# Attention values as paired 64-row matmuls in four accumulator banks, score and value units one by one, projection as one unit a block

## The chip, the cores and the metric

The kernel runs on one core of one Trainium2 chip. The metric is device time in microseconds (us). A quoted time is the median of a kernel's runs. Ratios are computed as the mean time of one kernel's runs over the mean of the other's runs of the same rounds, so they are not quite the ratio of the medians that are quoted.

Engines: PE is TensorE (PEld its weight loads), ACT is ScalarE, DVE is VectorE, POOL is GpSimd. Times inside an execution are read from the trace, in us from the start of the span.

## The reference

```python
xn = layernorm(x)                               # 2048 x 640
q  = (xn @ wq) as 32 heads of 192
p  = softmax(q @ k_cache.T * 192 ** -0.5)       # 2048 keys a head
s  = (p @ v_cache) @ wo
g  = silu(glu(xn))                              # w1, w3, w2; F = 1536
return x + s * g
```

Almost all the time is attention: 32 heads, each of four blocks of 512 queries, so 128 blocks. A block has eight units; unit `p` covers two groups of 128 keys, one from each half of the cache.

## The kernel before

For one unit, the scores are three rounds of two matmuls. The depth of 192 is cut in three pieces of 64 rows; the two matmuls of a round use rows 0 to 63 and 64 to 127 of the array, so they run at the same time. ScalarE takes the exponential of both in one instruction. A value matmul then uses all 128 rows (keys) and 193 columns; the 193rd is a column of ones, which gives the softmax sum.

```python
ps_st: 3 buffers of 128x1024 fp32   ps_o: 1 buffer of 128x1024   (512 columns are called a bank here: 2 each)
...
def emit_scores(h, qb, pairs):                      # pairs: four units
    for p in pairs:
        st2 = ps_st.tile([P, 1024], F32, tag="st2", name="st2")
        ...
        for r, (k0, q0, k1, q1) in enumerate(rounds):
            nc.tensor.matmul(st2[:, 0:512], lhsT=k0, rhs=q0, start=r == 0, stop=r == 2)      # rows 0..63
            nc.tensor.matmul(st2[:, 512:1024], lhsT=k1, rhs=q1, start=r == 0, stop=r == 2)   # rows 64..127
        nc.scalar.activation(out=pT2[:], in_=st2[:], func=ACT.Exp, scale=att_scale)
def values(n):
    for p, pT2 in zip(pairs, exps.pop(n)):
        for t in range(2):
            for j in range(4):
                nc.tensor.matmul(obank[:, j * 256:j * 256 + DH + 1],
                                 lhsT=pT2[:, t * 512 + j * P:t * 512 + (j + 1) * P],
                                 rhs=vt[:, t * NPAIR + p, 0:DH + 1], start=start, stop=stop)
    if not last: return
    nc.vector.reciprocal(out=rl, in_=ov[:, :, DH])
    nc.vector.tensor_tensor(out=ostage[...], in0=ov[:, :, 0:DH], in1=rl..., op=ALU.mult)
def project(h, qb, half):                           # queries of the next head, in a buffer of ps_st
    ...                                             # five matmuls of 128 rows, 512 columns
    nc.vector.tensor_copy(out=qAB[:, half, qs], in_=ps[:, 0:512])
```

In a block the order on TensorE is: scores of four units, values of the four before, half a projection, and the same again.

## Time and profile before

2048.06 us, median of 3 runs (2047.45 to 2048.43).

| reading | value | view |
|---|---|---|
| TensorE busy | 97% of the span | page, part 1 |
| chain that ended last | 97% TensorE | page, part 4 |
| one block, in the steady heads | 13.24 us | timeline (time between two evacuations) |
| exponential of one unit | 1.02 us, 0.91 us start to start | timeline |
| passages between 64-row and 128-row work | 510, of which 504 cost 92 to 97 ns | starts of matmuls in the trace |

The page of the kernel before, its parts 1 (busy us, share, instructions), 4 (chain by engine, then by line) and two groups of part 5 (busy, mean ns of one, idle before and its releaser):

```profile
span 2046.2 us, 39879 instructions
PE 1991.1 (97%) x17529; PEld 1282.7 (63%) x17777; DVE 485.7 (24%) x850; ACT 1031.5 (50%) x1145; POOL 337.0 (16%) x575
...
PE 97%; DMA 1%; issue 1%; DVE 1%; ACT 0%; POOL 0%; DVEq 0%; ACTq 0%; POOLq 0%
PE obank L364 35%; PE ps L292 13%; PE ps_s L102 10%; PE ps_f L503 3%; PE ps_gu L477 1%; PE ps_gu L474 1%; DMA KC<-KB 0%; DMA qC<-qAB 0%; PE pst L275 0%; DMA x_all<-in_A_x_dram 0%; DVE stats L257 0%; DVE xn L272 0%; DVE qAB L293 0%; PE st_238 L338 0%; PE st_256 L338 0%
...
L293 DVE CAST qAB<-ps 128x512 bf16<-128x512 f32 x256 | 175.7, 686 | 654.2 <-PE ps L292 654.2
L376 DVE TENSOR_TENSOR ostage<-obank,rl_all 128x768 bf16<-128x768 f32 x128 | 122.6, 958 | 4.4
```

TensorE is the limit, and VectorE is idle three quarters of the time: before its reciprocals and casts it waits for TensorE. The scaling L376 takes 958 ns and the projection's cast L293 686 ns.

The timeline of half a block (start, duration, engine, line, operation, count):

```profile
1002.30 0.37 PE L338 MATMUL st_12000<-qC,KC 64*128 64x512 bf16 x1
1002.32 0.38 PE L339 MATMUL st_12000<-qC,KC 64*128 64x512 bf16 x1
...
1002.63 0.61 PEld L364 LDWEIGHTS <-pT_11900 128*128 128x128 bf16 x8 [0.42 <-issue]
1002.63 0.84 PE L364 MATMUL obank<-vt_110,pT_11900 128*128 128x193 bf16 x8
...
1004.64 0.83 PE L364 MATMUL obank<-vt_110,pT_11927 128*128 128x193 bf16 x8
...
1005.31 1.24 PE L292 MATMUL ps<-xnT,wqB 128*128 128x512 bf16 x4
1006.48 0.09 PEld L338 LDWEIGHTS <-KA 64*128 64x128 bf16 x1 [0.42 <-issue]
...
1006.48 0.39 PE L338 MATMUL st_12050<-qAB,KA 64*128 64x512 bf16 x1
```

The last score round starts at 1002.32. Rounds follow each other after 0.215 us, so the next work could start at 1002.53; the first value matmul starts at 1002.63. The array passed from 64-row to 128-row work, and that cost about 96 ns. The 32 value matmuls from 1002.63 to 1005.31 take 83.7 ns each. Between the values and the projection, both of 128 rows, there is no gap. From the projection to the scores there is one again: projection matmuls start 216 ns apart, and the next score starts 312 ns after the last of them.

### The profile page before, as it was taken

The page shows a single profiled execution, that of the slowest core. Times are in us where ns is not written, and L with a number is a line of the kernel's source. Part 1 is how long each engine was busy: PE and PEld are TensorE (multiplying, and loading weights), DVE is VectorE, ACT ScalarE, POOL GpSimd, SP SyncE. Part 2 cuts the span into 40 slices and gives each one's busy share as a digit, 9 for nine tenths or more (in the row PEclk, how much of TensorE's full clock was granted, in tenths as well). Part 3 has the DMA queues.
Part 4 walks back from the last instruction along what each step waited for, and adds up shares of the span by engine and source line. Part 5 has one row for each costly group of instructions (what it writes and reads, how often), then busy time and mean ns, then how long its engine had stood idle before and what let it go on. Part 6 is the DMA issues. An engine that isn't in the chain of part 4 may idle for free.

```text
span 2046.2 us, 39879 instructions
## 1 busy us (share of the span) xinstructions
PE 1991.1 (97%) x17529; PEld 1282.7 (63%) x17777; DVE 485.7 (24%) x850; ACT 1031.5 (50%) x1145; POOL 337.0 (16%) x575
## 2 busy tenths in 40 slices
PE   5899999999999999999999999999999999999998
PEld 2466666666666666666666666666666666577776
DVE  3322222222222222222222222222222222521111
ACT  2556555655565565556555655555555566220000
POOL 2211111111111111111111111111111110000000
PEclk8999999999999999999999999999999999999999
DMA  8123232323343323244323323232323230928772
GB/s 152 34 63 97 65 97 65 95 59 94 66 97 66 95 66 97 63 122 104 96 65 78 82 56 87 64 96 60 93 58 93 63 88 8 235 50 149 149 148 55
DMA packets 361780, 177.40 MB, mean 87 GB/s; under 512 B 307584, under 2 KB 348288, under 8 KB 361600
## 3 DMA queue, kind: packets, MB, share of 16 engines
q1 hardware_dynamic: 335984, 114.96, 25.8%
q0 software_dynamic: 23312, 57.18, 11.4%
q10 hardware_dynamic: 2304, 2.62, 0.5%
q8 instruction: 141, 2.31, 0.5%
q14 instruction: 39, 0.32, 0.1%
HBM read 54.66 MB, written 27.79 MB: 40 GB/s over the span
## 4 chain that ended last, share of the span: by engine, by line
PE 97%; DMA 1%; issue 1%; DVE 1%; ACT 0%; POOL 0%; DVEq 0%; ACTq 0%; POOLq 0%
PE obank L364 35%; PE ps L292 13%; PE ps_s L102 10%; PE ps_f L503 3%; PE ps_gu L477 1%; PE ps_gu L474 1%; DMA KC<-KB 0%; DMA qC<-qAB 0%; PE pst L275 0%; DMA x_all<-in_A_x_dram 0%; DVE stats L257 0%; DVE xn L272 0%; DVE qAB L293 0%; PE st_238 L338 0%; PE st_256 L338 0%
## 5 line engine op out<-in xcount | busy, mean ns | idle before, releaser
L294 POOL DMA_DIRECT2D qC<-qAB x256 | 136.5, 533 | 1343.9 <-DVE qAB L293 1343.9
L293 DVE CAST qAB<-ps 128x512 bf16<-128x512 f32 x256 | 175.7, 686 | 654.2 <-PE ps L292 654.2
L338 PEld LDWEIGHTS <-KA 64*128 64x128 bf16 x1024 | 96.2, 94 | 198.2 <-issue 108.6
L102 PE MATMUL ps_s<-wo_sb,oT 128*128 128x256 bf16 (+1 forms) x1536 | 208.8, 299 | 0.0
L102 PEld LDWEIGHTS <-oT 128*128 128x128 bf16 x1536 | 150.2, 98 | 58.3
L375 DVE RECIPROCAL rl_all<-obank 128x4 f32<-128x4 f32 x128 | 23.4, 183 | 637.5 <-PE obank L364 637.5
L338 PEld LDWEIGHTS <-KC 64*128 64x128 bf16 x1024 | 96.2, 94 | 120.5 <-DMA KC<-KB 2.8
L292 PE MATMUL ps<-xnT,wqB 128*128 128x512 bf16 x516 | 153.5, 381 | 8.0 <-ACT xnT L277 1.3
L292 PE MATMUL ps<-xnT,wq 128*128 128x512 bf16 x520 | 153.4, 381 | 6.3
L338 PEld LDWEIGHTS <-KB 64*128 64x128 bf16 x1024 | 96.7, 94 | 61.3 <-issue 1.6
L339 PEld LDWEIGHTS <-KA 64*128 64x128 bf16 x1024 | 95.8, 94 | 49.9 <-issue 49.7
L376 DVE TENSOR_TENSOR ostage<-obank,rl_all 128x768 bf16<-128x768 f32 x128 | 122.6, 958 | 4.4
L339 PEld LDWEIGHTS <-KB 64*128 64x128 bf16 x1024 | 97.4, 95 | 17.9 <-issue 17.5
L339 PEld LDWEIGHTS <-KC 64*128 64x128 bf16 x1024 | 96.5, 94 | 0.4
L292 PEld LDWEIGHTS <-wqB 128*128 128x128 bf16 x640 | 61.0, 98 | 48.7 <-issue 3.6
L292 PEld LDWEIGHTS <-wq 128*128 128x128 bf16 x640 | 61.1, 98 | 48.0 <-issue 1.4
L296 POOL DMA_DIRECT2D qC<-qAB x128 | 67.1, 525 | 0.2 <-issue 0.2
L107 DVE SCALAR_TENSOR_TENSOR tmp<-ps_s,hT 128x384 f32<-128x384 f32 (+1 forms) x32 | 15.6, 488 | 177.4 <-PE ps_s L102 177.4
L503 PE MATMUL ps_f<-w_all,hT 128*128 128x384 bf16 (+1 forms) x384 | 52.3, 299 | 0.0
L98 POOL DMA_DIRECT2D xt<-in_A_x_dram x16 | 8.6, 540 | 253.2 <-DVE res L110 253.2
L503 PEld LDWEIGHTS <-hT 128*128 128x128 bf16 x384 | 37.6, 98 | 14.7
L308 DVE SCALAR_TENSOR_TENSOR hT<-pt,qAB 64x512 bf16<-64x512 bf16 x64 | 43.5, 679 | 1.0
(9261 smaller groups left out, 5305.6 us busy)
## 6 DMA issues: line engine op xcount, KB each, us to landing
qC<-qAB POOLq DMA_DIRECT2D x384, 64.0 KB, 1.9
o_scr<-ostage SPq DMA_DIRECT2D x16, 1536.0 KB, 9.8
vt_109<-in_A_v_cache_dram SPq DMA_DIRECT2D x16, 768.0 KB, 5.5
vt_110<-in_A_v_cache_dram SPq DMA_DIRECT2D x16, 768.0 KB, 5.3
wq<-in_A_wq_dram POOLq DMA_DIRECT2D x32, 240.0 KB, 3.5
wo_sb<-in_A_wo_dram POOLq DMA_DIRECT2D x1, 7680.0 KB, 37.4
KC<-KA POOLq DMA_DIRECT2D x32, 128.0 KB, 5.2
KC<-KB POOLq DMA_DIRECT2D x32, 128.0 KB, 5.3
```

Of the source, the lines that this page charges most:

```text
L102: nc.tensor.matmul(ps[:, b * 512:b * 512 + c1 - c0], lhsT=oT[:, k, :], rhs=wo_sb[:, k, c0:c1], start=(k == 0), stop=(k == OC - 1))
L292: nc.tensor.matmul(ps[:, 0:512], lhsT=w, rhs=xnT[:, c, qs], start=(c == 0), stop=(c == DC - 1))
L293: nc.vector.tensor_copy(out=qAB[:, half, qs], in_=ps[:, 0:512])
L294: nc.gpsimd.dma_start(out=qC[0:64, half, qs], in_=qAB[64:P, half, qs])
L296: nc.gpsimd.dma_start(out=qC[64:P, 0, qs], in_=qAB[0:64, 0, qs])
L308: nc.vector.scalar_tensor_tensor(out=hid, in0=t[:], scalar=1.0, in1=z, op0=ALU.add, op1=ALU.mult)
L338: nc.tensor.matmul(st2[:, 0:512], lhsT=k0, rhs=q0, start=r == 0, stop=r == 2)
L339: nc.tensor.matmul(st2[:, 512:1024], lhsT=k1, rhs=q1, start=r == 0, stop=r == 2)
L364: nc.tensor.matmul(obank[:, j * 256:j * 256 + DH + 1], lhsT=pT2[:, t * 512 + j * P:t * 512 + (j + 1) * P], rhs=vt[:, t * NPAIR + p, 0:DH + ...
L375: nc.vector.reciprocal(out=rl, in_=ov[:, :, DH])
L376: nc.vector.tensor_tensor(out=ostage[:, qb * 4:qb * 4 + 4, hg * DH:(hg + 1) * DH], in0=ov[:, :, 0:DH], in1=rl.unsqueeze(2).to_broadcast([P ...
L503: nc.tensor.matmul(ps[:, b * 512:b * 512 + c1 - c0], lhsT=hT[:, fc, i * P:(i + 1) * P], rhs=w2_sb[:, fc, c0:c1], start=(fc == 0), stop=(fc ...
```

## The change

The intent: if the values also run as 64-row tiles, two at a time, the array passes between the modes only around the projection. The Trainium skill (TensorEngine Tiling (Array Packing), Gotcha 1: PSUM Pressure) says that different row tiles write different PSUM banks and can't access the same one at the same time, so each row half gets its own two accumulator banks. The accumulator then has four banks instead of two, and the scores have four instead of six: two buffers instead of three. At the end of a block the two halves have to be added.

```diff
-    pp = ...(name="pp", bufs=10)
+    pp = ...(name="pp", bufs=6)
+    osp = ...(name="osp", bufs=2)
-    ps_st = ...(name="ps_st", bufs=3, PSUM)
+    ps_st = ...(name="ps_st", bufs=2, PSUM)
 def project(h, qb, half):
-        nc.vector.tensor_copy(out=qAB[:, half, qs], in_=ps[:, 0:512])
+        if half:
+            nc.scalar.copy(out=qAB[:, 1, qs], in_=ps[:, 0:512])
+        else:
+            nc.vector.tensor_copy(out=qAB[:, 0, qs], in_=ps[:, 0:512])
 def values(n):                                   # n is now one unit, not four
-            obanks[0] = ps_o.tile([P, 1024], F32, tag="ob", name="obank")
+            obanks[0] = ps_o.tile([P, 2048], F32, tag="ob", name="obank")
-                    nc.tensor.matmul(obank[:, j * 256:j * 256 + DH + 1], lhsT=pT2[:, ...], rhs=vt[:, ...], ...)
+                for r in range(2):
+                    o0 = r * 1024 + j * 256
+                    nc.tensor.matmul(obank[:, o0:o0 + DH + 1],
+                                     lhsT=pT2[r * 64:(r + 1) * 64, ...], rhs=vt[r * 64:(r + 1) * 64, ...], ...)
+        nc.scalar.copy(out=osum[:], in_=ov[:, 0, :, 0:DH + 1])
+        nc.vector.tensor_tensor(out=osum[:], in0=ov[:, 1, :, 0:DH + 1], in1=osum[:], op=ALU.add)
-        nc.vector.reciprocal(out=rl, in_=ov[:, :, DH])
+        nc.vector.reciprocal(out=rl, in_=osum[:, :, DH])
         nc.vector.tensor_tensor(out=ostage[...], in0=osum..., in1=rl..., op=ALU.mult)
 ...
+    for n, (h, qb, p) in enumerate(stream):
+        scores(n + 2)
+        values(n)
         ...
+            if p == NPAIR - 1:                   # end of the block
+                project(h + 1, qb, 1)
+                project(h + 1, qb, 0)
```

The cut leaves out two smaller edits: in head 0 the layer norm and the head's own projection stand at other units, and the weights of the head after next are loaded one block later.

More of the change, by code (lines that the diff above doesn't have):

```diff
@@ L185, in _kernel_impl @@
     qlp = att.enter_context(tc.tile_pool(name="qlp", bufs=2))
-    pp = att.enter_context(tc.tile_pool(name="pp", bufs=10))
+    pp = att.enter_context(tc.tile_pool(name="pp", bufs=6))
     stp = att.enter_context(tc.tile_pool(name="stp", bufs=1))
     hbp = att.enter_context(tc.tile_pool(name="hbp", bufs=2))
+    osp = att.enter_context(tc.tile_pool(name="osp", bufs=2))
     lnp = att.enter_context(tc.tile_pool(name="lnp", bufs=2))
-    ps_st = main.enter_context(tc.tile_pool(name="ps_st", bufs=3, space=bass.MemoryType.PSUM))
+    ps_st = main.enter_context(tc.tile_pool(name="ps_st", bufs=2, space=bass.MemoryType.PSUM))
     ps_o = main.enter_context(tc.tile_pool(name="ps_o", bufs=1, space=bass.MemoryType.PSUM))
@@ L310, in swiglu, with emit_scores @@
             nc.vector.scalar_tensor_tensor(out=hid, in0=hid, scalar=0.5, in1=z, op0=ALU.mult, op1=ALU.mult)
-    NG = -(-NPAIR // 4)
-    gsz = [NPAIR // NG + (1 if g < NPAIR % NG else 0) for g in range(NG)]
-    stream = []
-    for h in range(H):
-        for qb in range(NQB):
-            p0 = 0
-            for g in range(NG):
-                stream.append((h, qb, list(range(p0, p0 + gsz[g])), g == 0, g == NG - 1))
-                p0 += gsz[g]
-    def emit_scores(h, qb, pairs):
+    stream = [(h, qb, p) for h in range(H) for qb in range(NQB) for p in range(NPAIR)]
+    def emit_scores(h, qb, p):
         L = loads[h]
@@ L328, in emit_scores @@
         qs = slice(qb * 512, (qb + 1) * 512)
-        pts = []
-        for p in pairs:
-            lo = slice(p * P, (p + 1) * P)
-            hi = slice(HK + p * P, HK + (p + 1) * P)
-            st2 = ps_st.tile([P, 1024], F32, tag="st2", name="st2")
-            rounds = [(KA[0:64, lo], qAB[0:64, 0, qs], KA[64:P, hi], qAB[64:P, 0, qs]),
-                      (KB[0:64, lo], qC[0:64, 0, qs], KB[64:P, hi], qAB[64:P, 1, qs]),
-                      (KC[0:64, lo], qC[0:64, 1, qs], KC[64:P, lo], qC[64:P, 0, qs])]
-            for r, (k0, q0, k1, q1) in enumerate(rounds):
-                nc.tensor.matmul(st2[:, 0:512], lhsT=k0, rhs=q0, start=r == 0, stop=r == 2)
-                nc.tensor.matmul(st2[:, 512:1024], lhsT=k1, rhs=q1, start=r == 0, stop=r == 2)
-            pT2 = pp.tile([P, 1024], BF16, tag="pT2", name="pT2")
-            nc.scalar.activation(out=pT2[:], in_=st2[:], func=ACT.Exp, scale=att_scale)
-            pts.append(pT2)
-        return pts
+        lo = slice(p * P, (p + 1) * P)
+        hi = slice(HK + p * P, HK + (p + 1) * P)
+        st2 = ps_st.tile([P, 1024], F32, tag="st2", name="st2")
+        rounds = [(KA[0:64, lo], qAB[0:64, 0, qs], KA[64:P, hi], qAB[64:P, 0, qs]),
+                  (KB[0:64, lo], qC[0:64, 0, qs], KB[64:P, hi], qAB[64:P, 1, qs]),
+                  (KC[0:64, lo], qC[0:64, 1, qs], KC[64:P, lo], qC[64:P, 0, qs])]
+        for r, (k0, q0, k1, q1) in enumerate(rounds):
+            nc.tensor.matmul(st2[:, 0:512], lhsT=k0, rhs=q0, start=r == 0, stop=r == 2)
+            nc.tensor.matmul(st2[:, 512:1024], lhsT=k1, rhs=q1, start=r == 0, stop=r == 2)
+        pT2 = pp.tile([P, 1024], BF16, tag="pT2", name="pT2")
+        nc.scalar.activation(out=pT2[:], in_=st2[:], func=ACT.Exp, scale=att_scale)
+        return pT2
     exps = {}
@@ L350, in scores @@
     def scores(n):
-        exps[n] = emit_scores(*stream[n][:3])
+        if n < len(stream):
+            exps[n] = emit_scores(*stream[n])
     def values(n):
-        h, qb, pairs, first, last = stream[n]
-        if first:
-            obanks[0] = ps_o.tile([P, 1024], F32, tag="ob", name="obank")
+        h, qb, p = stream[n]
+        if p == 0:
+            obanks[0] = ps_o.tile([P, 2048], F32, tag="ob", name="obank")
         obank = obanks[0]
         vt = loads[h]["vt"]
-        for p, pT2 in zip(pairs, exps.pop(n)):
-            for t in range(2):
-                for j in range(4):
-                    start = p == 0 and t == 0 and j % 2 == 0
-                    stop = p == NPAIR - 1 and t == 1 and j % 2 == 1
-                    nc.tensor.matmul(obank[:, j * 256:j * 256 + DH + 1],
-                                     lhsT=pT2[:, t * 512 + j * P:t * 512 + (j + 1) * P],
-                                     rhs=vt[:, t * NPAIR + p, 0:DH + 1], start=start, stop=stop)
-        if not last:
+        pT2 = exps.pop(n)
+        for t in range(2):
+            for j in range(4):
+                start = p == 0 and t == 0 and j % 2 == 0
+                stop = p == NPAIR - 1 and t == 1 and j % 2 == 1
+                for r in range(2):
+                    o0 = r * 1024 + j * 256
+                    nc.tensor.matmul(obank[:, o0:o0 + DH + 1],
+                                     lhsT=pT2[r * 64:(r + 1) * 64, t * 512 + j * P:t * 512 + (j + 1) * P],
+                                     rhs=vt[r * 64:(r + 1) * 64, t * NPAIR + p, 0:DH + 1], start=start, stop=stop)
+        if p < NPAIR - 1:
             return
@@ L372, in values @@
         ostage = ostages[0]
-        ov = obank[:].rearrange("p (j w) -> p j w", j=4)
+        ov = obank[:].rearrange("p (r j w) -> p r j w", r=2, j=4)
+        osum = osp.tile([P, 4, DH + 1], F32, tag="osum", name="osum")
+        nc.scalar.copy(out=osum[:], in_=ov[:, 0, :, 0:DH + 1])
+        nc.vector.tensor_tensor(out=osum[:], in0=ov[:, 1, :, 0:DH + 1], in1=osum[:], op=ALU.add)
         rl = rl_all[:, h * NQT + qb * 4:h * NQT + qb * 4 + 4]
-        nc.vector.reciprocal(out=rl, in_=ov[:, :, DH])
-        nc.vector.tensor_tensor(out=ostage[:, qb * 4:qb * 4 + 4, hg * DH:(hg + 1) * DH], in0=ov[:, :, 0:DH],
+        nc.vector.reciprocal(out=rl, in_=osum[:, :, DH])
+        nc.vector.tensor_tensor(out=ostage[:, qb * 4:qb * 4 + 4, hg * DH:(hg + 1) * DH], in0=osum[:, :, 0:DH],
                                 in1=rl.unsqueeze(2).to_broadcast([P, 4, DH]), op=ALU.mult)
     def loads_after(h, qb):
-        if qb == 1 and h + 2 < H:
+        if qb == max(1, NQB - 2) and h + 2 < H:
             load_w(h + 2)
@@ L421, in _kernel_impl @@
     load_v(1)
-    for n, (h, qb, pairs, first, last) in enumerate(stream):
-        if h == 0 and last and qb + 1 < NQB:
-            values(n)
-            project(0, qb + 1, 1)
-            project(0, qb + 1, 0)
-            if qb + 2 < NQB:
-                ln_stats(qb + 2)
-            scores(n + 1)
-        else:
-            if n + 1 < len(stream):
-                scores(n + 1)
-            values(n)
-            if h == 0 and first and qb + 1 < NQB:
-                ln_norm(qb + 1)
-        if first and h + 1 < H and h > 0:
-            project(h + 1, qb, 1)
-        if last:
-            if h + 1 < H:
-                if h == 0:
-                    project(1, qb, 1)
-                    if qb == 0:
-                        copy_k(1)
+    scores(1)
+    for n, (h, qb, p) in enumerate(stream):
+        scores(n + 2)
+        values(n)
+        if h == 0 and qb + 1 < NQB:
+            if p == 0 and qb > 0:
+                ln_stats(qb + 1)
+            if p == NPAIR // 2 - 1:
+                ln_norm(qb + 1)
+            if p == NPAIR - 3:
+                project(0, qb + 1, 1)
+                project(0, qb + 1, 0)
+        if h + 1 < H:
+            if h == 0 and qb == 0 and p == NPAIR - 1:
+                copy_k(1)
+            if p == NPAIR - 1:
+                project(h + 1, qb, 1)
                 project(h + 1, qb, 0)
+        if p == NPAIR - 1:
             if h < 2 * NPIG:
```

## The prediction

> **What bounds the kernel now.** TensorE. The page's first part has PE busy for 97% of the span, and the chain that ended last is 97% PE (values 35%, projection 13%). The attention part, from about 47 us to about 1743 us, is 128 blocks of (head, 512 queries). The timeline view shows heads of 52.96 us, so 13.24 us a block. ScalarE's exponentials (1.02 us each, 0.91 us start to start when back to back) and VectorE (24% busy) have slack.
>
> One block, from starts in the timeline: 24 score pairs (two 64-row matmuls, starts 4 ns apart, next pair 0.215 us later) = 5.17 us; 64 value matmuls (128 rows, 193 columns) at 0.083 us = 5.3 us; 10 projection matmuls at 0.2155 us = 2.16 us. Each passage between 64-row and 128-row work costs 96 ns extra (308 ns instead of 213 from score to value, 312 instead of 216 from projection to score); a block has four: 0.38 us. The rest, about 0.2 us, is mostly the fourth score pair of a group waiting for one of three score buffers. The Trainium skill (TensorEngine Tiling (Array Packing), Key Properties) says that a change of tiling mode drains TensorE; this trace agrees, at 96 ns.
>
> **What the change does.**
> - Value matmuls become twice as many, in 64-row pairs. If pairs overlap as the score pairs do, a pair costs what one matmul cost, 0.083 us: no gain, no loss.
> - Four passages a block become two: -0.19 us. No group of four runs into the score buffers: -0.2 us. The ideal block is 12.8 us, about 55 us less in all.
> - Added: ScalarE copies half the accumulator (128x772; estimated 0.8 us from the exponential's rate), VectorE adds the other half (about 0.96 us, as the present 128x768 operation), then reciprocal, the scaling (0.9 us) and the cast of the second projection (0.68 us).
> - Score buffers go from three to two, and the projection takes both. The score pair after next then waits for VectorE's cast, which is in order behind add, reciprocal and scaling. Counted from the block's last value pair: copy ends at about 1.4 us, add 2.4, reciprocal 2.6, scaling 3.5, cast 4.2. PE wants the buffer at about 3.75 us. I expect a stall of 0.3 to 0.6 us a block, all on the critical path: 40 to 75 us. That gives the gain back.
>
> **The risk.** One element (score and value pair) is 44 TensorE instructions in 1.31 us, 30 ns each. The trace shows 41 ns sustained (values) and 28 ns only in bursts of 20 (transposes). The Trainium skill (TensorE: Matmul & The Clock Gate, Wait — 56ns, not 53.3ns?) gives about 62 ns a matmul when the sequencer decodes by microcode. If issue can't keep 30 ns, value pairs cost more, in full on the path: at 35 ns about 230 us. I give it three chances in ten.
>
> **Prediction.** 2048 us - 55 + 55, so about 2050 us; range 2012 to 2150. Faster by over 2%: 0.14. Within 2%: 0.58. Slower by over 2%: 0.28.
>
> **What the profile would show.** Starts of successive value pairs 83 ns apart, the two of a pair about 4 ns (issue limit: more than 100 ns, with weight loads late by "issue"). No 96 ns gap between scores and values, two a block around the projection. In the waits, the second score pair after a projection waiting on VectorE's cast for 0.3 to 0.6 us, about 124 times. Exponentials never on the chain. Output stage unchanged.
>
> **What would make it wrong.** Row tiles at 193 columns that don't overlap, or instruction issue (slower, up to 15%); a VectorE sequence that ends before 3.75 us, so that no stall appears (1995 us, faster); a longer one.

## The result, and the profile after

The changed kernel takes 2078.94 us (median of 4 runs, 2076.0 to 2082.4) against 2048.21 us: ratio 1.0151, 95% interval 1.0134 to 1.0169. It is 1.5% slower, within the stated range and in the class "within 2%".

The page of the changed kernel, the same parts:

```profile
span 2077.2 us, 56883 instructions
PE 1980.5 (95%) x25838; PEld 1350.0 (65%) x25969; DVE 520.1 (25%) x850; ACT 1279.7 (62%) x1401; POOL 336.7 (16%) x575
...
PE 69%; DVE 16%; ACT 7%; issue 6%; DMA 1%; ACTq 0%; DVEq 0%; POOL 0%
PE obank L361 25%; PE ps_s L102 10%; DVE osum L373 6%; ACT osum L372 5%; DVE ostage L376 4%; DVE qAB L297 4%; PE ps_f L499 3%; DVE rl_all L375 1%; PE ps_gu L470 1%; PE ps_gu L473 1%; PE ps L293 1%; DVE stats L258 0%; DMA KC<-KB 0%; DMA qC<-qAB 0%; ACT xnT L278 0%
...
L373 DVE TENSOR_TENSOR osum<-obank,osum 128x772 f32<-128x772 f32 x128 | 123.1, 962 | 1264.4 <-ACT osum L372 1264.4
L376 DVE TENSOR_TENSOR ostage<-osum,rl_all 128x768 bf16<-128x768 f32 x128 | 122.6, 958 | 4.4
L372 ACT COPY osum<-obank 128x772 f32<-128x772 f32 x128 | 101.9, 796 | 0.9 <-PE obank L361 0.9
L297 DVE CAST qAB<-ps 128x512 bf16<-128x512 f32 x128 | 87.5, 683 | 23.5 <-PE ps L293 23.5
```

The share of TensorE in the chain fell from 97% to 69%. VectorE has 16% and ScalarE 7% of the chain now, although VectorE is still busy for only a quarter of the span. The lines that appear are those of a block's end: copy L372, add L373, scaling L376, cast L297.

The chain of waits around one block's end (start, duration, what). The block's last value pair started at 1009.68:

```profile
1010.29 0.81 ACT osum L372
1011.10 0.02 issue
1011.12 0.97 DVE osum L373
1012.09 0.02 issue
1012.12 0.19 DVE rl_all L375
1012.30 0.02 issue
1012.33 0.96 DVE ostage L376
1013.28 0.61 DVE qAB L297
1013.90 0.04 issue
1013.94 0.37 PE st_16741 L332
```

Each piece released the next: ScalarE's copy of the first half, VectorE's add of the second, reciprocal, scaling, cast, and then the score matmul L332. The times after the last value pair are 1.41 us (copy ends), 2.40, 2.62, 3.61 and 4.21 us (cast ends).

The timeline at the end of that chain:

```profile
1013.21 0.68 DVE L297 CAST qAB<-ps 128x512 bf16<-128x512 f32 x1
1013.38 0.09 PEld L332 LDWEIGHTS <-KA 64*128 64x128 bf16 x1
...
1013.94 0.37 PE L332 MATMUL st_16741<-qAB,KA 64*128 64x512 bf16 x1 [0.32 <-DVE qAB L297]
1013.94 0.09 PEld L333 LDWEIGHTS <-KA 64*128 64x128 bf16 x1 [0.47 <-issue]
```

TensorE's previous value pair started at 1013.38, and a score round normally follows a value pair after 80 ns, at 1013.46. It started at 1013.94, when the cast of the projection had freed its buffer. That is 0.48 us lost. (The bracket says 0.32 us, because the profile models the end of the last matmul; the start-to-start distance is the one that counts.) The list of waits, which the prediction had named as the place to look, shows the stall in 124 lines, because the score buffers there carry numbers: 122 of 0.3 us and two of 0.6, about 38 us in all. A short list hides them. One of them (total us, times, longest) is `PE st_28421 L332 <- DVE qAB L297: 0.3, 1, 0.3`.

Over the whole trace, the second score unit after a projection starts 560 ns (median) after the value pair before it, instead of 80, in the 124 cases at the end of a block; in the four cases in which head 0 projects for itself the distances are 52 to 398 ns. The excess adds up to 60.1 us. The array passes between 64-row and 128-row work 262 times instead of 510. Value pairs start 83 ns apart, as single value matmuls did before.

Where the 31.0 us between the two profiled spans (2046.2 and 2077.2) came from, by the starts of each block's last value matmul in both traces (the scaling would be no fair mark: it starts 0.50 us after that matmul in the kernel before and 2.64 us after it in the changed kernel):

| stretch | before | after | difference |
|---|---|---|---|
| start to the end of the fifth block | 124.5 | 126.2 | +1.7 |
| 119 steady blocks | 1576.1 | 1592.5 | +16.4 |
| the last blocks (head 31) | 42.5 | 48.8 | +6.3 |
| after the last value matmul | 303.1 | 309.7 | +6.6 |

In head 31 there is no projection to do. There TensorE reaches the next block's first value pair before the add has emptied the single accumulator, as a line of the changed kernel's list of waits shows (total us, times, longest):

```profile
PE obank L361 <- DVE osum L373: 4.6, 3, 1.5
```

By the starts of matmuls these three waits cost 1.72 us each, 5.2 us in all: the first value pairs of two units lie 3.04 us apart there instead of 1.31. Besides, the kernel before runs four units of scores ahead of the values and the changed one two; so two units of scores (1.3 us) moved from the first stretch of the table to this one.

### The profile page after: what moved, and what is told of

Its sections match the earlier page's. It is cut to its first block, busy times and chain, and to the rows that moved or that the text cites. A ratio compares the mean times of both kernels' runs of the same rounds, so it can differ in the third digit from the quotient of the medians.

```text
span 2077.2 us, 56883 instructions
## 1 busy us (share of the span) xinstructions
PE 1980.5 (95%) x25838; PEld 1350.0 (65%) x25969; DVE 520.1 (25%) x850; ACT 1279.7 (62%) x1401; POOL 336.7 (16%) x575
## 3 DMA queue, kind: packets, MB, share of 16 engines
q10 hardware_dynamic: 2304, 2.62, 0.5%
## 4 chain that ended last, share of the span: by engine, by line
PE 69%; DVE 16%; ACT 7%; issue 6%; DMA 1%; ACTq 0%; DVEq 0%; POOL 0%
PE obank L361 25%; PE ps_s L102 10%; DVE osum L373 6%; ACT osum L372 5%; DVE ostage L376 4%; DVE qAB L297 4%; PE ps_f L499 3%; DVE rl_all L375 1%; PE ps_gu L470 1%; PE ps_gu L473 1%; PE ps L293 1%; DVE stats L258 0%; DMA KC<-KB 0%; DMA qC<-qAB 0%; ACT xnT L278 0%
## 5 line engine op out<-in xcount | busy, mean ns | idle before, releaser
L373 DVE TENSOR_TENSOR osum<-obank,osum 128x772 f32<-128x772 f32 x128 | 123.1, 962 | 1264.4 <-ACT osum L372 1264.4
L332 PEld LDWEIGHTS <-KC 64*128 64x128 bf16 x1024 | 96.3, 94 | 111.4 <-DMA KC<-KB 4.5
L293 PE MATMUL ps<-xnT,wq 128*128 128x512 bf16 x640 | 159.4, 380 | 0.0
L332 PEld LDWEIGHTS <-KA 64*128 64x128 bf16 x1024 | 96.3, 94 | 58.3 <-issue 54.2
L376 DVE TENSOR_TENSOR ostage<-osum,rl_all 128x768 bf16<-128x768 f32 x128 | 122.6, 958 | 4.4
L372 ACT COPY osum<-obank 128x772 f32<-128x772 f32 x128 | 101.9, 796 | 0.9 <-PE obank L361 0.9
L332 PEld LDWEIGHTS <-KB 64*128 64x128 bf16 x1024 | 96.5, 94 | 0.3 <-issue 0.3
L293 PEld LDWEIGHTS <-wqB 128*128 128x128 bf16 x640 | 52.4, 98 | 67.6 <-issue 22.0
L297 DVE CAST qAB<-ps 128x512 bf16<-128x512 f32 x128 | 87.5, 683 | 23.5 <-PE ps L293 23.5
L295 ACT CAST qAB<-ps 128x512 bf16<-128x512 f32 x128 | 75.1, 586 | 13.8 <-PE ps L293 4.7
```

The lines of the kernel that those rows point to most:

```text
L293: nc.tensor.matmul(ps[:, 0:512], lhsT=w, rhs=xnT[:, c, qs], start=(c == 0), stop=(c == DC - 1))
L295: nc.scalar.copy(out=qAB[:, 1, qs], in_=ps[:, 0:512])
L297: nc.vector.tensor_copy(out=qAB[:, 0, qs], in_=ps[:, 0:512])
L372: nc.scalar.copy(out=osum[:], in_=ov[:, 0, :, 0:DH + 1])
L373: nc.vector.tensor_tensor(out=osum[:], in0=ov[:, 1, :, 0:DH + 1], in1=osum[:], op=ALU.add)
L376: nc.vector.tensor_tensor(out=ostage[:, qb * 4:qb * 4 + 4, hg * DH:(hg + 1) * DH], in0=osum[:, :, 0:DH], in1=rl.unsqueeze(2).to_broadcast( ...
```

## The experiments

Theory A: the row tiles are free, and the loss is the stall of a score buffer behind VectorE's sequence at the end of a block. Theory B: the value pairs themselves cost, through twice the matmuls, four banks or instruction issue. The last of the eight kernels computes wrong values. The record marks all eight results as correct, that one too, so its check does not notice such an error in the values.

| kernel | median us | runs | ratio to before, same rounds | steady block, us |
|---|---|---|---|---|
| before | 2048.21 | 4 | 1 | 13.24 |
| changed | 2078.94 | 4 | 1.0151 | 13.38 |
| both casts on ScalarE | 2016.99 | 4 | 0.9842 | 12.88 |
| scaling after the cast | 2016.35 | 4 | 0.9835 | 12.88 |
| scaling twice | 2202.66 | 2 | 1.0745 | 14.37 |
| values at 128 rows | 2238.93 | 2 | 1.0922 | 14.66 |
| three buffers after attention | 2074.13 | 4 | 1.0110 | 13.38 |
| scaling after the cast + three buffers | 2014.42 | 5 | 0.9817 | 12.88 |
| the same + head 0 earlier | 2001.94 | 5 | 0.9760 | 12.88 |
| values of 97 columns (wrong result) | 1742.28 | 1 | one look | 10.67 |

### Both casts on ScalarE

```diff
-        if half:
-            nc.scalar.copy(out=qAB[:, 1, qs], in_=ps[:, 0:512])
-        else:
-            nc.vector.tensor_copy(out=qAB[:, 0, qs], in_=ps[:, 0:512])
+        nc.scalar.copy(out=qAB[:, half, qs], in_=ps[:, 0:512])
```

> The changed kernel with one edit: both casts of the projection on ScalarE. Theory A (the stall is VectorE's chain add, reciprocal, scaling, cast, which holds the second score buffer; the trace of the changed kernel shows PE idle about 0.48 us there in each of 124 blocks): the cast no longer stands behind the scaling and ends near 3.2 us after the last value pair, before PE wants the buffer at 3.8. The stall goes, block 13.38 to 12.9 us, time 2079 to about 2019 us. Theory B (the loss comes from the value pairs: twice the matmuls, four banks, 44 instructions in an element): moving a cast changes nothing, 2079 within 5 us.

Measured: 2016.99 us, block 12.88 us. The second score unit after a projection starts 80 ns after its value pair; the excess over the trace is zero. Theory A holds, theory B does not.

### Scaling after the cast

```diff
+        def scale():
-        nc.vector.reciprocal(out=rl, in_=osum[:, :, DH])
-        nc.vector.tensor_tensor(out=ostage[...], in0=osum..., in1=rl..., op=ALU.mult)
+            nc.vector.reciprocal(out=rl, in_=osum[:, :, DH])
+            nc.vector.tensor_tensor(out=ostage[...], in0=osum..., in1=rl..., op=ALU.mult)
+        return scale
 ...
                 project(h + 1, qb, 0)
         if p == NPAIR - 1:
+            scale()
```

(`values(n)` now returns `scale`; that line is cut.)

> The changed kernel with one edit: reciprocal and scaling are issued after the projection's cast on VectorE, no work moved to another engine. Theory A (VectorE's order holds the score buffer): the cast ends about 1.1 us earlier, the stall goes, about 2019 us, as with the cast on ScalarE. Theory B (value pairs themselves): 2079 within 5 us. If only ScalarE's load mattered, this one would stay at 2079 while the cast on ScalarE moved.

Measured: 2016.35 us, block 12.88 us. No work was taken from VectorE; its busy time is 519.6 us against 520.1. Only the order differs. The timeline of VectorE at a block's end now reads:

```profile
1001.17 0.96 DVE L373 TENSOR_TENSOR osum<-obank,osum 128x772 f32<-128x772 f32 x1 [9.40 <-ACT osum L372]
...
1002.29 0.69 DVE L297 CAST qAB<-ps 128x512 bf16<-128x512 f32 x1 [0.15 <-PE ps L293]
...
1002.90 0.17 DVE L377 RECIPROCAL rl_all<-osum 128x4 f32<-128x4 f32 x1
...
1003.10 0.96 DVE L378 TENSOR_TENSOR ostage<-osum,rl_all 128x768 bf16<-128x768 f32 x1
```

The add starts at 1001.17 and the cast follows at 1002.29. It waits 0.15 us for the projection's last matmul, and reciprocal and scaling come behind it, where nobody waits for them. The chain of this kernel is TensorE's again:

```profile
PE 96%; DVE 2%; DMA 1%; issue 1%; ACT 0%; POOL 0%; DVEq 0%; ACTq 0%
PE obank L361 34%; PE st L332 33%; PE ps L293 14%; PE ps_s L102 10%; PE ps_f L503 3%; PE ps_gu L474 1%; PE ps_gu L477 1%; PE st L333 1%; DVE stats L258 0%; DMA KC<-KB 0%; DMA qC<-qAB 0%; ACT xnT L278 0%; DMA x_all<-in_A_x_dram 0%; PE pst L276 0%; DVE qAB L297 0%
```

### Scaling twice

```diff
         nc.vector.tensor_tensor(out=ostage[...], in0=osum..., in1=rl..., op=ALU.mult)
+        nc.vector.tensor_tensor(out=ostage[...], in0=osum..., in1=rl..., op=ALU.mult)
```

> The changed kernel with the scaling on VectorE done twice (same result). Theory A: everything that VectorE does before the cast is on the critical path, so all of the added 0.96 us shows in each of 124 blocks: stall 0.48 to 1.44 us, block 13.38 to 14.34 us, time about 2198 us. Theory B: VectorE is 25% busy and has slack; no change, 2079 within 5 us.

Measured: 2202.66 us. The block grew from 13.38 to 14.37 us, that is by the whole of the added operation (0.99 us start to start), and the excess at the second score unit from 60.1 to 183.0 us. On an engine that is a quarter busy, the whole of an operation placed ahead of the cast is on the critical path here.

### Values at 128 rows, still one by one

```diff
-                for r in range(2):
-                    o0 = r * 1024 + j * 256
-                    nc.tensor.matmul(obank[:, o0:o0 + DH + 1], lhsT=pT2[r * 64:(r + 1) * 64, ...],
-                                     rhs=vt[r * 64:(r + 1) * 64, ...], start=start, stop=stop)
+                o0 = t * 1024 + j * 256
+                nc.tensor.matmul(obank[:, o0:o0 + DH + 1], lhsT=pT2[:, ...], rhs=vt[:, ...],
+                                 start=start, stop=stop)
```

> The changed kernel with the value matmuls at 128 rows again (64 instead of 128 a block, the two key halves into the two bank pairs, so that the evacuation stays the same), score and value units still one by one. Theory A (a passage between 64 and 128 rows costs 96 ns): 16 passages a block instead of 2, +1.34 us, of which about 0.1 us takes the place of the stall: block about 14.6 us, time about 2239 us. Theory B (the doubled number of instructions is what costs): faster than 2079 us.

Measured: 2238.93 us, block 14.66 us, 2044 passages between 64-row and 128-row work instead of 262. Half the value matmuls, and 160 us slower. (The stall's total fell from 60.1 to 47.6 us, because TensorE arrives later at the buffer, as expected.) The timeline shows a passage on each side of the eight value matmuls of a unit:

```profile
1003.48 0.38 PE L333 MATMUL st<-qC,KC 64*128 64x512 bf16 x1
1003.78 0.61 PEld L360 LDWEIGHTS <-pT 128*128 128x128 bf16 x8 [0.42 <-issue]
1003.79 0.84 PE L360 MATMUL obank<-vt,pT 128*128 128x193 bf16 x8
...
1004.56 0.09 PEld L332 LDWEIGHTS <-KA 64*128 64x128 bf16 x1 [0.16 <-issue]
```

From the last score round (1003.48) to the first value matmul there are 308 ns instead of 212, and from the last value matmul to the next score 179 ns instead of 83. So the order "one by one" needs the values in the score's mode, and a passage costs 96 ns in this order too (92 to 97 ns in 1906 of the 2044; the others coincide with another wait).

### Three score buffers after the attention part

The last stages share the score buffers, so they also fell from three to two.

```diff
-    ps_st = main.enter_context(tc.tile_pool(name="ps_st", bufs=2, PSUM))
-    ps_o = main.enter_context(...)
+    ps_st = att.enter_context(tc.tile_pool(name="ps_st", bufs=2, PSUM))
+    ps_o = att.enter_context(...)
 ...
     att.close()
+    ps_st = main.enter_context(tc.tile_pool(name="ps_t", bufs=3, PSUM))
```

> The changed kernel with one edit: after the attention part its PSUM pools are closed and a pool of three score buffers is opened for the last stages, as the kernel before had (during attention there are still two). The last stages of the changed kernel took 301.9 us from the first gate matmul to the last output matmul, against 295.4. Theory: two buffers instead of three cost this; time 2079 to about 2072.5 us. Rival: the 6.5 us is chance of the run (its runs spread over 6 us); no change.

Measured: 2074.13 us, ratio 1.0110 with the interval 1.0094 to 1.0125, against 1.0151 (1.0134 to 1.0169) of the changed kernel. The trace is sharper than the totals. From the first gate matmul to the last output matmul it shows 295.42 us (295.43 before, 301.91 in the changed kernel), so the loss in these stages is all due to the missing third buffer. It is no chance of one run: the traces of the five other experiments that keep two buffers there show 300.3 to 301.9 us. But the new pool's first matmul starts 2.1 us after the last value matmul instead of 0.2. The trace names what it waited for, the last block's add, which empties the accumulator:

```profile
1772.49 1.24 PE L471 MATMUL ps_gu<-xnT,w_all 128*128 128x512 bf16 x5 [1.89 <-DVE osum L373]
```

The net gain in the trace is then about 4.5 us, less than I expected. The chain at the passage to the output stage, in the changed kernel:

```profile
1804.86 52.29 PE ps_f L499 x384
1857.14 0.11 PE cnt L509
1857.25 2.14 issue
1859.40 2.69 PE ps_s L102 x10
```

And in this one, with no gap of 2.14 us:

```profile
1807.19 52.16 PE ps_f L500 x384
1859.35 0.10 PE cnt L510
1859.44 2.71 PE ps_s L102 x16
```

### Both repairs

> Scaling after the cast, and three buffers after the attention part. Theory: the two costs are in different stages and add; 2016 to about 2010 us, 1.9% under the kernel before.

Measured: 2014.42 us, ratio 0.9817, where the scaling after the cast alone had 0.9835. The intervals (0.9803 to 0.9830 and 0.9819 to 0.9851) overlap a little, so the totals alone hardly separate the two; the last stages are 295.42 us in this trace too, and the delay of 2.1 us at their start is there as well. It is short of the 2010 us that I expected.

### Head 0 earlier

In head 0 the layer norm and the head's own projection stand between the attention units, and the trace of the kernel with the scaling after the cast shows TensorE waiting: in two blocks the first transposes start 2.15 us after the value matmul before them, and in three blocks the first two score rounds after the projection start 1.17 us and 2.1 to 2.2 us after what precedes them.

```diff
-            if p == 0 and qb > 0:
-                ln_stats(qb + 1)
-            if p == NPAIR // 2 - 1:
+            if p == NPAIR // 2 and qb + 2 < NQB:
+                ln_stats(qb + 2)
+            if p == 0:
                 ln_norm(qb + 1)
-            if p == NPAIR - 3:
+            if p == 2:
                 project(0, qb + 1, 1)
                 project(0, qb + 1, 0)
```

> As the kernel with both repairs, and in head 0 the layer norm's statistics, transposes and the next block's projection are issued some elements earlier (statistics half a block, transposes at the block's first element, projection at its third), so that TensorE no longer waits there. Head 0's blocks take 23.9 us in three cases where work for about 16.5 is there; I expect 12 to 18 us less, about 1995 us, so over 2% faster than the kernel before.

Measured: 2001.94 us, ratio 0.9760 (0.9747 to 0.9773), faster than the kernel before. It is 12.5 us under the kernel with both repairs. The kernel before has the waits after the projection too (1.16 us, and 2.1 us in two blocks and 5.3 us in the third), but not the one before the first transposes: they start 0.08 us after the value matmul before them. This edit was not tried on the kernel before, so how much of the 2.4% is the change's own is not shown.

### Values of 97 columns: how fast can TensorE be fed?

```diff
+                    c0 = 0 if p == 0 else DH // 2
-                    nc.tensor.matmul(obank[:, o0:o0 + DH + 1], lhsT=..., rhs=vt[..., 0:DH + 1], ...)
+                    nc.tensor.matmul(obank[:, o0 + c0:o0 + DH + 1], lhsT=..., rhs=vt[..., c0:DH + 1], ...)
```

> A measurement with a wrong result on purpose: the kernel with scaling after the cast, its value matmuls cut to 97 columns in seven of eight elements. Question: can TensorE's issue keep more than the present 44 instructions in 1.31 us (30 ns each)? If issue is no limit, a value pair falls from 83 to about 43 ns, an element to about 0.99 us (22 ns an instruction), a block from 12.88 to about 10.6 us, time about 1730 us. If issue is at its limit near 30 ns, the time stays near 2016 us.

Measured in one look (state unknown, wrong result on purpose): 1742.28 us, block 10.67 us. The timeline of TensorE:

```profile
999.89 0.52 PE L362 MATMUL obank<-vt,pT 64*128 64x97 bf16 x16
1000.24 0.38 PE L332 MATMUL st<-qAB,KA 64*128 64x512 bf16 x1
...
1000.89 0.52 PE L362 MATMUL obank<-vt,pT 64*128 64x97 bf16 x16
1001.24 0.37 PE L332 MATMUL st<-qAB,KA 64*128 64x512 bf16 x1
```

A unit (score and value) takes 1.00 us, and the 16 value matmuls of eight pairs take 0.35 us from first start to the next score, 43 ns a pair. With the weight loads that are 44 instructions in 1.00 us, 22.7 ns each. So at the 30 ns of the changed kernel the issue of instructions was not a limit. This rests on one run, but the question was whether the rate can be reached at all.

## Why the prediction was right

- **The bound.** TensorE was the limit of the kernel before, as predicted, and in both kernels that lose the stall by one edit it is again (96% of the chain with both casts on ScalarE and with the scaling after the cast).
- **Value pairs cost what one matmul cost.** Right: 83 ns a pair, start to start. The two of a pair start about 3 ns apart in some stretches and 18 to 20 ns apart in others. In the changed kernel the larger offset begins at the score unit that waits and lasts until the next projection, and it does not lengthen the pair's period. The kernel with the scaling after the cast, without that wait, stays at about 3 ns in the steady blocks. The Trainium skill (TensorE: Matmul & The Clock Gate, Part 3, The mechanism) gives about 4 ns between the starts; here that is only the smaller of two values.
- **Passages.** Right: 510 became 262, and a passage costs about 96 ns in all kernels.
- **The size of the gain.** Mis-sized. I expected an ideal block of 12.8 us and 55 us in all. The block without the stall takes 12.88 us, so 0.36 us less than before; over the 119 steady blocks (13.245 to 12.884 us on average) that is 43 us. Two passages are 0.19 us of it. Most of the rest is the groups of four: in the kernel before, units inside a group start 0.671 us apart on average, where three rounds of 0.2155 us need 0.647, six times a block: 0.14 us. This split is worked out from the starts; no experiment takes the two apart.
- **The stall.** Right in place, in cause and in size: I expected the cast to end 4.2 us after the last value pair where TensorE wants the buffer at 3.75, a stall of 0.3 to 0.6 us a block and 40 to 75 us in all. The trace has 4.21 us, 3.79 us, 0.48 us and 60.1 us. Both kernels that move the cast ahead of the scaling lose the stall, and the one that doubles the scaling enlarges it by the whole operation. The list of waits has it as predicted, 124 times and 0.3 to 0.6 us each. One detail of the profile did not hold: exponentials were never to stand on the chain, and 33 of them do, each for about 1.02 us; what they cost is not shown.
- **What the sum left out.** "Output stage unchanged" was wrong. The last stages share the pool that went from three buffers to two; their matmuls took 6.5 us more, and three buffers brought exactly that back. Head 31 without projections took 6.3 us more: 5.2 us are TensorE's waits for the add that empties the single accumulator, and 1.3 us are scores that moved there from the start; no experiment takes that apart, it rests on the trace. The first five blocks took 1.7 us more; what of that is the change is open, since this stretch took from 120.2 to 129.0 us in the four experiments that changed neither head 0 nor the length of a unit or block end for the worse.
- **The sum.** Predicted 2048 - 55 + 55, measured +31. From the parts: -43 for the cheaper steady blocks, +59 for their stall (13.38 - 12.88 us, 119 times), and 14.6 for the three stretches that the sum did not have. That the measured time lies 29 us above the predicted 2050 and still in the range is partly luck: the range held it because the risk of slow issue had stretched its upper end; that risk, to which I gave three chances in ten, did not come, and the run with 97 columns shows that it was not near.

## What to carry to other kernels

Halving the passages of the array between tiling modes did gain 0.36 us a block, together with the end of the groups of four; but with two score buffers left, the sequence of a mostly idle engine at a block's end came onto the critical path, and a quarter-busy VectorE then cost more than the gain. (No run kept three score buffers during the attention part, so whether the third alone would have hidden the sequence is not shown.) When a change takes a buffer away, write down the sequence that frees each remaining one, in the order in which its engine will run it, and put whatever frees a buffer for the busiest engine ahead of work that nobody waits for: the same instructions in another order were worth about 3% here (ratio 1.0151 against 0.9835). Look also at every stage that shares the pool, not only at the one that the change is about.

## What the Trainium skill lacked or had wrong

- TensorEngine Tiling (Array Packing), Key Properties: it says that changing the mode drains TensorE, but gives no size. Here a change between 64-row and 128-row work costs 92 to 97 ns, in 504 of 510, 253 of 262 and 1906 of 2044 passages of three kernels; the others coincide with another wait.
- TensorE: Matmul & The Clock Gate, Wait — 56ns, not 53.3ns?: the page ties its 62 ns a matmul to decoding by microcode; it is not wrong, but does not say how to tell from a profile which decoding is in force. No limit of 62 ns shows in these runs. With values of 97 columns a unit's 22 matmuls took 1.00 us, 45 ns each, throughout the attention part (a block with its projection has 186 matmuls in 10.67 us, 57 ns each).
- TensorE: Matmul & The Clock Gate, Part 3, The mechanism: about 4 ns between the starts of two row tiles. The changed kernel shows about 3 ns or, from the unit that waits to the next projection, 18 to 20 ns (7125 of its 8192 pairs lie between 17 and 21 ns), at no cost to the period of 83 ns.
- TensorEngine Tiling (Array Packing), PSUM Bottleneck: it says that the copy out of PSUM may become the bottleneck once tiling has made TensorE four times as fast, and advises to use both ScalarE and VectorE. Here the sequence at a block's end became a limit although the value matmuls gained nothing (83 ns a pair, as one matmul before) and both engines were in use; the two row halves double what is to be evacuated, and the order of the instructions on VectorE decided (2078.94 against 2016.35 us).
